# Block-sorted attention and a gated MLP on one core: the next batch's attention woven into this batch's gMLP in a fixed order

## The chip, the cores and the metric

The kernel runs on one core of a Trainium2 chip. The metric is the device time of one execution in microseconds. Before the change the median of three runs is 314.42 us (314.01 to 315.52).

## What is computed

Four batches, 8 heads, 768 tokens, head width 64; the tokens of a head form 8 blocks of 96. An 8x8 matrix per head (`sort_net`, after five rounds of exp and row and column scaling) mixes the blocks of K and of V. Each block of Q then attends to its mixed block. The heads side by side are the input x (768x512) of a gated MLP with a spatial matrix over the tokens.

```python
for _ in range(5):
    P = np.exp(P - np.max(P, axis=-1, keepdims=True))
    P = P / np.sum(P, -1, keepdims=True);  P = P / np.sum(P, -2, keepdims=True)
k_sorted = np.einsum('bhij,bhjcd->bhicd', P, k_b);  v_sorted = ...   # the same for v
attn = softmax(scale * q_b @ k_sb.T)          # 96x96 in each of the 8 blocks
x = (attn @ v_sb) as [batch, token, head*64]
h = np.maximum(x @ w_in, 0.0);  u, v = h[..., :512], h[..., 512:]
v_n = (v - mean(v)) / np.sqrt(var(v) + 1e-06)
v_s = np.einsum('ts,bsd->btd', w_spatial, v_n) + b_spatial[None, :, None]
out = (u * v_s) @ w_out
```

## The kernel before

**Layout.** A head's 768 tokens lie as 128 partitions of 6 tokens (token 6p+g in partition p, chunk g). With 96 = 16 x 6, a block is 16 partitions in all 6 chunks, so mixing the blocks is one matmul per chunk against a 128x128 matrix `pdiag` (32 of them, built on GpSimd at L192). The tile framework sorts the instructions of every engine by its own estimate of times; nothing in the code fixes the order. There are two PSUM pools (L67, L68): `ps2` with 2 buffers of two banks, `ps1` with 4 buffers of one bank.

**Start.** Weights are loaded first, on the GpSimd queue with a cast to bf16 (L116 to L131), then the heads. `w_spatial` is transposed on TensorE (L139, copies at L144). The 5 scaling rounds run on ScalarE and VectorE (L157 to L167).

**Attention of a batch (L223 to L284), head by head.** Three loads of 96 KB (L217, 128 rows of 1536 bytes in fp32 each). Six transposes of Q into `qt_ps` (L232, 64 partitions) and a copy that puts the tokens into block order (L236, VectorE). Six matmuls mix and transpose K (L240) and ScalarE copies them (L246). Six matmuls mix V (L250), VectorE copies (L257), and V goes to DRAM (L260) and comes back with a block's 96 tokens on partitions (L265, rows of 128 bytes); SyncE issues both. Eight matmuls of 64x96 by 96 columns give the scores (L272), ScalarE takes exp of all (L279). No maximum is subtracted.

**Softmax sums (L286 to L300).** Sixteen matmuls over the heads collect the sums of all 8 heads on 8 partitions (L289, L293). Two reciprocals on VectorE invert them (L299 512 wide, L300 256 wide). For each pair of heads two matmuls spread them over 128 partitions (L306, L308), ScalarE copies (L311), 16 matmuls of P·V in pairs on the two column halves of the array (L315, L321) give x transposed, and VectorE multiplies (L328) into `xt`.

**gMLP of the batch.** Per 128 tokens: v half of x·w_in (L340, 4 matmuls of 512 columns), relu (L347, ScalarE), mean and variance (L350, L351, VectorE). Then `rstd` through Ln and Exp on ScalarE (L354, L356), and 6 normalisations (L359, VectorE). Per 128 features: u (L370), relu (L377), spatial product and bias (L382, L388), gate (L396, VectorE). Per 128 tokens: output projection (L402), copy (L409, ScalarE), store (L410, SyncE).

```python
recip = small.tile([H, S], BF16, tag="recip")
nc.vector.reciprocal(out=recip[:, 0:512], in_=rs_a)
...
nc.scalar.activation(out=rstd, in_=mv_tile[:, :, 1], func=AF.Ln, bias=eps_tile[:], scale=1.0)
nc.scalar.activation(out=rstd, in_=rstd, func=AF.Exp, bias=0.0, scale=-0.5)
```

Of the kernel before, what the change touches and what calls it, by code (L numbers as in the profile page):

```python
# [21 lines left out]


@with_exitstack
def kernel(
# [17 lines left out]
    G = S // 128  # L44
    BH = B * H
# [22 lines left out]
    ps1 = ctx.enter_context(tc.tile_pool(name="ps1", bufs=4, space=bass.MemoryType.PSUM))  # L68
# [18 lines left out]
        out=sel16.rearrange("p (j t) -> p j t", t=16),  # L87
        in_=sel16.rearrange("p (j t) -> p j t", t=16),
        pattern=[[1, NB], [0, 16]], compare_op=ALU.not_equal,
        fill=1.0, base=0, channel_multiplier=-1,  # L90
    )

    selh = const.tile([BLK, H, H], BF16)
    nc.gpsimd.memset(selh, 0.0)
    nc.gpsimd.affine_select(
        out=selh, in_=selh, pattern=[[1, H], [-1, H]], compare_op=ALU.not_equal,
        fill=1.0, base=0, channel_multiplier=0,
    )

    ibc = const.tile([8, H * 64], BF16)  # L100
    nc.gpsimd.memset(ibc, 0.0)
    nc.gpsimd.affine_select(
        out=ibc.rearrange("p (h r) -> p h r", r=64),
        in_=ibc.rearrange("p (h r) -> p h r", r=64),
        pattern=[[1, H], [0, 64]], compare_op=ALU.not_equal,
        fill=1.0, base=0, channel_multiplier=-1,
    )

    ones_bf = const.tile([128, 128], BF16)
    nc.gpsimd.memset(ones_bf, 1.0)  # L110
# [5 lines left out]
    nc.gpsimd.dma_start(  # L116
        out=w_in_sb,
        in_=moe_w_in.rearrange("(kc p) f -> p kc f", p=128),
    )
    wsp_nat = pers.tile([128, SC, S], BF16)  # L120
    nc.gpsimd.dma_start(
        out=wsp_nat,
        in_=moe_w_spatial.rearrange("(tc p) s -> p tc s", p=128),
    )
    w_out_sb = pers.tile([128, FC, DM], BF16)
    nc.gpsimd.dma_start(
        out=w_out_sb,
        in_=moe_w_out.rearrange("(fc p) n -> p fc n", p=128),
    )
    b_sb = pers.tile([1, S], BF16)  # L130
    nc.gpsimd.dma_start(  # L131
        out=b_sb, in_=moe_b_spatial.rearrange("(a s) -> a s", a=1),
    )

    wspT = pers.tile([128, SC, S], BF16)
    for sc in range(SC):
        tp = ps1.tile([128, S], BF16, name="wspT_ps", tag="a")
        for tci in range(SC):
            nc.tensor.transpose(  # L139
                tp[:, tci * 128:(tci + 1) * 128],  # L140
                wsp_nat[:, tci, sc * 128:(sc + 1) * 128],
                ident_bf,
            )
        nc.vector.tensor_copy(out=wspT[:, sc, :], in_=tp)  # L144

    mask16_ps = ps1.tile([128, 128], FP32, name="mask16_ps", tag="a")
    nc.tensor.matmul(mask16_ps, lhsT=a16, rhs=a16, start=True, stop=True)
    mask16 = const.tile([128, 128], BF16)
    nc.vector.tensor_copy(out=mask16, in_=mask16_ps)

    p_all = pers.tile([BH, NB, NB], FP32)
    nc.sync.dma_start(out=p_all, in_=sort_net.rearrange("b h i j -> (b h) i j"))
# [30 lines left out]
    prep_ps = ps1.tile([128, NB * BH], FP32, name="prep_ps", tag="a")
    nc.tensor.matmul(prep_ps, lhsT=sel16, rhs=pt_sb, start=True, stop=True)
    prep_sb = pers.tile([128, NB * BH], BF16)
    nc.vector.tensor_copy(out=prep_sb, in_=prep_ps)

    pdiags = []
    for bh in range(BH):
        pd = pdiag_pool.tile([128, 128], BF16, name="pdiag")  # L190
        in1 = _raw_ap(prep_sb, bh, [prep_sb.ap[0], [BH, NB], [0, 16]])
        nc.gpsimd.tensor_mul(  # L192
            out=pd.rearrange("p (i t) -> p i t", t=16),
            in0=mask16.rearrange("p (i t) -> p i t", t=16),
            in1=in1,
        )
        pdiags.append(pd)

    def perm_in_ap(x: bass.AP, b: int, h: int) -> bass.AP:
        base = (b * H + h) * S * D  # L200
        return _raw_ap(x, base, [[6 * D, 128], [D, G], [1, D]])

    def blockview(ap, i):
        return ap[:, i * BLK:(i + 1) * BLK]

    def chunk2block(ap):
        return ap.rearrange("p (m j t) -> p j t m", m=G, j=NB, t=16)

    def natview(ap):
        return ap.rearrange("p (j t m) -> p j t m", j=NB, t=16, m=G)  # L210

    def expview(ap, i):
        return ap.rearrange("p (i c) -> p i c", c=BLK)[:, i, :]

    def load_perm(x: bass.AP, b: int, h: int, name: str, tag: str) -> bass.AP:
        t = att_in.tile([128, G, D], BF16, name=name, tag=tag)
        nc.gpsimd.dma_start(out=t, in_=perm_in_ap(x, b, h))  # L217
        return t

    for b in range(B):  # L220
        exp_tiles = []
        vblk_tiles = []
        for h in range(H):  # L223
            bh = b * H + h
            parity = h % 2
            q_perm = load_perm(q, b, h, "q_perm", "q")
            k_perm = load_perm(k, b, h, "k_perm", "k")
            v_perm = load_perm(v, b, h, "v_perm", "v")

            qt_ps = ps1.tile([64, G * 128], BF16, name="qt_ps", tag="a")  # L230
            for g in range(G):
                nc.tensor.transpose(  # L232
                    qt_ps[:, g * 128:(g + 1) * 128], q_perm[:, g, :], ident_bf,
                )
            qt_sb = att_mid.tile([64, S], BF16, name="qt_sb", tag="qt")
            nc.vector.tensor_copy(out=natview(qt_sb), in_=chunk2block(qt_ps))  # L236

            kt_ps = ps2.tile([64, S], FP32, name="kt_ps", tag="a")
            for g in range(G):
# [203 lines left out]
```

## Time and profile before

| | before |
|---|---|
| median of 3 runs | 314.42 us |
| span of the profiled execution | 313.4 us (its own time is given by no other number) |
| TensorE busy | 236.8 us, 76% |
| VectorE / ScalarE / GpSimd busy | 130.2 / 115.5 / 69.1 us |
| mean granted TensorE clock | 0.804 |
| chain that ended last | TensorE 61%, ScalarE 11%, VectorE 10%, DMA 8%, GpSimd 6% |

The span runs from the first to the last instruction; the run's time lies some 1 us above it. The granted clock is a share of 2.4 GHz; its two levels are 1.0 (2.4 GHz) and 0.5 (1.2 GHz), and a number between is a mean over the stretch. "Busy" of TensorE counts matmuls whose ends are modelled, so the time between the starts of neighbours says more than the duration of one.

### The profile page before, as it was taken

Reading aid. Unit: us, or ns where it says so; the run is one execution under the profiler, and the core shown is the slowest. Engines: PE = TensorE matmul, PEld = TensorE weight load, DVE = VectorE, ACT = ScalarE, POOL = GpSimd, SP = SyncE. Lnnn points to the kernel's source line nnn. Section 1 sums busy time; section 2 is a strip of 40 time slices with the busy share of each in tenths; the row PEclk is TensorE's granted clock in tenths of the full one; section 3 lists DMA queues with packets and bytes.
Section 4 is the critical chain, followed back from the end, with each engine's and each line's share of the span. In section 5 each row is a group of like instructions: output and inputs, shape, how many; then the busy total and the mean of one; then the engine's idle time right before and its main releaser. Section 6 shows DMA issues by size and latency. Waiting matters only on the chain.

```text
span 313.4 us, 4510 instructions
## 1 busy us (share of the span) xinstructions
PE 236.8 (76%) x1783; PEld 126.6 (40%) x1783; DVE 130.2 (42%) x216; ACT 115.5 (37%) x166; POOL 69.1 (22%) x149
## 2 busy tenths in 40 slices
PE   0058379489499997497699984794999983986994
PEld 0056265234144574143244762241445751432441
DVE  4345341533512382726321854536123917262220
ACT  2003333234512576126223664327125761353114
POOL 9239986100000285000000771000002100000000
PEclk9995955556779999658799997567799995586799
DMA  2996499400000599500001999100005950000005
GB/s 36 206 201 111 79 170 216 69 2 0 0 0 2 205 196 216 91 0 0 0 2 60 247 200 172 32 2 0 0 0 200 176 105 0 2 1 0 0 2 201
DMA packets 48917, 25.08 MB, mean 80 GB/s; under 512 B 27648, under 2 KB 45312, under 8 KB 48896
## 3 DMA queue, kind: packets, MB, share of 16 engines
q0 software_dynamic: 15696, 12.20, 26.1%
q1 hardware_dynamic: 33200, 12.60, 15.4%
q8 instruction: 14, 0.23, 0.3%
q14 instruction: 7, 0.06, 0.0%
HBM read 27.54 MB, written 9.44 MB: 118 GB/s over the span
## 4 chain that ended last, share of the span: by engine, by line
PE 61%; ACT 11%; DVE 10%; DMA 8%; POOL 6%; issue 2%; DVEq 0%; ACTq 0%; POOLq 0%
PE vst_ps L382 13%; PE v_ps L340 10%; PE ut_ps L370 7%; PE o_ps L402 7%; DMA w_out_sb<-in_moe_w_out_dram 5%; PE sc_ps L272 5%; DVE recip L299 4%; POOL pdiag L192 4%; PE vst_ps L388 3%; PE qt_ps L232 3%; PE ot_ps L315 3%; PE kt_ps L240 2%; ACT kt_sb L246 2%; ACT exp_sb L279 2%; PE rs_a L289 2%
## 5 line engine op out<-in xcount | busy, mean ns | idle before, releaser
L382 PE MATMUL vst_ps<-wspT,v_sb 128*128 128x512 bf16 (+1 forms) x192 | 46.1, 371 | 18.5 <-DVE v_sb L359 17.9
L217 POOL DMA_DIRECT2D q_perm<-in_q_dram x32 | 17.9, 560 | 156.1 <-PE qt_ps L232 153.0
L279 ACT ACTIVATE exp_sb<-sc_ps 96x768 bf16<-96x768 f32 x32 | 25.8, 806 | 36.7 <-PE sc_ps L272 36.7
L236 DVE COPY qt_sb<-qt_ps 64x768 bf16<-64x768 bf16 x32 | 30.2, 945 | 19.7 <-PE qt_ps L232 19.6
L396 DVE TENSOR_TENSOR gt_sb<-vst_ps,ut_sb 128x768 bf16<-128x768 f32 x16 | 15.3, 958 | 53.2 <-PE vst_ps L388 53.2
L382 PEld LDWEIGHTS <-v_sb 128*128 128x128 bf16 x192 | 19.4, 108 | 39.5 <-DVE v_sb L359 22.8
L340 PE MATMUL v_ps<-w_in_sb,xt 128*128 128x512 bf16 x96 | 35.1, 512 | 0.0
L377 ACT ACTIVATE ut_sb<-ut_ps 128x768 bf16<-128x768 f32 x16 | 13.0, 810 | 56.4 <-PE ut_ps L370 56.4
L246 ACT CAST kt_sb<-kt_ps 64x768 bf16<-64x768 f32 x32 | 25.1, 784 | 16.9 <-PE kt_ps L240 16.8
L370 PE MATMUL ut_ps<-xt,w_in_sb 128*128 128x512 bf16 (+1 forms) x128 | 31.2, 363 | 0.0
L311 ACT CAST bc_sb<-bc_ps 128x768 bf16<-128x768 f32 x16 | 12.8, 799 | 41.7 <-PE bc_ps L308 41.7
L328 DVE TENSOR_TENSOR xt<-ot_ps,bc_sb 128x768 bf16<-128x768 f32 x16 | 15.3, 958 | 28.4 <-PE ot_ps L321 23.2
L299 DVE RECIPROCAL recip<-rs_a 8x512 bf16<-8x512 f32 x4 | 13.4, 3346 | 26.1 <-PE rs_a L289 26.1
L257 DVE CAST vperm_sb<-vperm_ps 128x384 bf16<-128x384 f32 x32 | 17.4, 544 | 14.1 <-PE vperm_ps L250 8.7
L272 PE MATMUL sc_ps<-qt_sb,kt_sb 64*96 64x96 bf16 x256 | 19.7, 223 | 4.0 <-ACT kt_sb L246 3.5
L306 PE MATMUL bc_ps<-recip,ibc 8*128 8x512 bf16 x16 | 9.4, 591 | 16.6 <-DVE recip L299 13.1
L402 PE MATMUL o_ps<-w_out_sb,gt_sb 128*128 128x512 bf16 x96 | 21.4, 379 | 0.0
L315 PEld LDWEIGHTS <-vblk_sb 96*64 96x64 bf16 x128 | 10.9, 161 | 24.2 <-issue 24.2
L272 PEld LDWEIGHTS <-kt_sb 64*96 64x96 bf16 x256 | 15.5, 133 | 11.5 <-ACT kt_sb L246 9.1
L232 PE MATMUL qt_ps<-ident_bf,q_perm 128*64 128x128 bf16 x192 | 19.2, 239 | 1.0 <-DMA q_perm<-in_q_dram 1.0
L409 ACT COPY o_sb<-o_ps 128x512 f32<-128x512 f32 x24 | 13.7, 586 | 17.1 <-PE o_ps L402 17.1
L217 POOL DMA_DIRECT2D k_perm<-in_k_dram x32 | 17.7, 554 | 10.1 <-PE kt_ps L240 5.5
(73 smaller groups left out, 307.9 us busy)
## 6 DMA issues: line engine op xcount, KB each, us to landing
out_dram<-o_sb SPq DMA_DIRECT2D x24, 256.0 KB, 2.2
q_perm<-in_q_dram POOLq DMA_DIRECT2D x32, 96.0 KB, 4.9
k_perm<-in_k_dram POOLq DMA_DIRECT2D x32, 96.0 KB, 4.9
v_perm<-in_v_dram POOLq DMA_DIRECT2D x32, 96.0 KB, 4.9
vdram<-vperm_sb SPq DMA_DIRECT2D x32, 96.0 KB, 3.7
vblk_sb<-vdram SPq DMA_DIRECT2D x32, 96.0 KB, 3.1
wsp_nat<-in_moe_w_spatial_dram POOLq DMA_DIRECT2D x1, 1152.0 KB, 13.2
w_in_sb<-in_moe_w_in_dram POOLq DMA_DIRECT2D x1, 1024.0 KB, 8.6
```

Source lines behind the costliest of these rows:

```text
L217: nc.gpsimd.dma_start(out=t, in_=perm_in_ap(x, b, h))
L232: nc.tensor.transpose(qt_ps[:, g * 128:(g + 1) * 128], q_perm[:, g, :], ident_bf,)
L236: nc.vector.tensor_copy(out=natview(qt_sb), in_=chunk2block(qt_ps))
L246: nc.scalar.copy(out=natview(kt_sb), in_=chunk2block(kt_ps))
L272: nc.tensor.matmul(sc_ps[:, i, 0:BLK], lhsT=blockview(kt_sb, i), rhs=blockview(qt_sb, i), start=True, stop=True,)
L279: nc.scalar.activation(out=exp_sb.rearrange("p (i c) -> p i c", c=BLK), in_=sc_ps[:, :, 0:BLK], func=AF.Exp, scale=scale,)
L299: nc.vector.reciprocal(out=recip[:, 0:512], in_=rs_a)
L315: nc.tensor.matmul(ot_ps[0:64, i, 0:BLK], lhsT=vblk_tiles[2 * m][:, i, :], rhs=expview(exp_tiles[2 * m], i), start=True, stop=True,)
L340: nc.tensor.matmul(v_ps, lhsT=xt_tiles[kc][:, sc * 128:(sc + 1) * 128], rhs=w_in_sb[:, kc, DH:DFF], start=(kc == 0), stop=(kc == KC - 1),)
L370: nc.tensor.matmul(ut_ps[:, off:off + wdt], lhsT=w_in_sb[:, kc, mc * 128:(mc + 1) * 128], rhs=xt_tiles[kc][:, off:off + wdt], start=(kc == ...
L382: nc.tensor.matmul(vst_ps[:, off:off + wdt], lhsT=v_tiles[sc][:, mc * 128:(mc + 1) * 128], rhs=wspT[:, sc, off:off + wdt], start=(sc == 0) ...
L402: nc.tensor.matmul(o_ps, lhsT=gt_tiles[mc][:, sc * 128:(sc + 1) * 128], rhs=w_out_sb[:, mc, :], start=(mc == 0), stop=(mc == FC - 1),)
```

## The change

The kernel is rewritten, with the same mathematics.

- **Order.** `attention(b)` is a list of 28 units, `gmlp(b)` one of 14. Inside `manual_schedule` TensorE, VectorE and ScalarE run their instructions in the order in which the code issues them. First comes `attention(0)` alone, with the six transposes of `w_spatial` as units between its last ones. Then for every batch each gMLP unit is followed by two (at places three) attention units of the next batch. The last gMLP stands alone. GpSimd and SyncE are still sorted by the framework.
- **PSUM.** One pool of 4 buffers of two banks; every unit takes one buffer.
- **Loads.** Per batch one DMA for V, one for K (1024 rows of 1536 bytes each) and six for Q (1024 rows of 256 bytes each, as tokens x heads). Batch 0 is loaded ahead of the weights, batch 1 behind them, batch b+2 when stage b is issued.
- **Token order.** Q stays in the permuted order; blocks are picked by strided views (`block_cols`). `w_spatial`, the bias and the output rows are permuted in the same way.
- **Attention.** Two heads share a transpose (12 transposes of 128x128 per `qtr`) and a `ktr` (12 matmuls in column pairs). V is mixed by 8 matmuls of 384 columns, gets a column of ones per head (65 wide) and makes one round trip through DRAM per batch: one store, six reads (rows of 1040 bytes). `attend` gives x with tokens on partitions and the sum in column 64; VectorE takes 8 reciprocals per partition and multiplies. `xtr` transposes x on TensorE.
- **gMLP.** Two 128-token chunks share one PSUM buffer and one relu or copy (1024 wide); u and spatial products go in 384-column halves; the bias matmul has 128 rows instead of 1.
- **ScalarE.** One activation table set is named at the start (`preload_act_table_set`).

```diff
+    nc.scalar.preload_act_table_set("natural_log_exp_and_others")
+    def load_tokens(x, b, name):
+        t = ld.tile([128, G, H, D], BF16, name=name, tag=name)
+        for g in range(G):
+            nc.gpsimd.dma_start(
+                out=t[:, g],
+                in_=_raw_ap(x, b * H * S * D + g * D, [[G * D, 128], [S * D, H], [1, D]]),
+            )
...
+        def vmix(hp):
+            t = ps_tile()
+            for hh in range(2):
                 nc.tensor.matmul(
+                    t[:, hh, 0:G * D], lhsT=pd[:, 2 * hp + hh, :], rhs=v_in[:, 2 * hp + hh, :],
+                    start=True, stop=True,
                 )
...
+        def attend(n):
...
+            for hh in range(2):
+                for ii in range(NB // 2):
+                    i = ih * (NB // 2) + ii
+                    nc.tensor.matmul(
+                        t[0:BLK, hh, ii * VW:(ii + 1) * VW],
+                        lhsT=e[:, hh, ii, :], rhs=st["vb"][:, i, 2 * hp + hh, :],
+                        start=True, stop=True,
+                    )
+            tv = t[0:BLK, :, 0:NB // 2 * VW].rearrange("p h (i d) -> p h i d", d=VW)
+            rec = small.tile([BLK, 2, NB // 2], FP32, name="rec", tag="rec")
+            nc.vector.reciprocal(out=rec, in_=tv[:, :, :, D])
+            nc.vector.tensor_mul(
...
+        order = [
+            (vmix, 0), (vmix, 1), (vmix, 2), (vmix, 3), (qtr, 0), (ktr, 0), (qtr, 1), (ktr, 1),
+            (score, 0), (ktr, 2), (score, 1), (ktr, 3), (attend, 0), (score, 2), (attend, 1),
+            (score, 3), (attend, 2), (score, 4), (attend, 3), (score, 5), (attend, 4), (score, 6),
+            (xtr, 0), (attend, 5), (score, 7), (attend, 6), (attend, 7), (xtr, 1),
+        ]
...
+        order = (
+            [(vproj, n) for n in range(3)] + [(uproj, n) for n in range(FC)]
+            + [(spatial, n) for n in range(FC)] + [(oproj, n) for n in range(3)]
+        )
...
+    with tc.manual_schedule(engines=ORDERED):
...
+        for b in range(B):
+            if b + 2 < B:
+                load_batch(b + 2)
+            m_units = gmlp(b)
+            a_units = attention(b + 1) if b + 1 < B else []
+            done = 0
+            for n, unit in enumerate(m_units):
+                unit()
+                want = min(len(a_units), (n + 1) * 28 // 13)
+                while done < want:
+                    a_units[done]()
+                    done += 1
```

## Rows read from the trace of the kernel before

**Rows 1.** The page, busy time of each engine.

```profile
PE 236.8 (76%) x1783; PEld 126.6 (40%) x1783; DVE 130.2 (42%) x216; ACT 115.5 (37%) x166; POOL 69.1 (22%) x149
```

**Rows 2.** Windows: stretch and length, busy per engine, PEclk, DMA share, GB/s.

```profile
41.20:57.70 16.50, 15.52 (x115) 10.27 (x116) 4.34 (x6) 7.20 (x9) 10.67 (x21) 0.50 1.27 195
...
107.00:125.60 18.60, 16.20 (x223) 11.91 (x220) 11.06 (x16) 12.46 (x17) 12.70 (x24) 1.00 1.22 214
125.60:133.80 8.20, 3.54 (x39) 1.85 (x37) 5.92 (x3) 1.60 (x2) 0.00 (x0) 0.58 0.44 80
133.80:144.60 10.80, 10.80 (x58) 4.05 (x57) 3.37 (x4) 2.72 (x5) 0.00 (x0) 0.53 0.00 0
144.60:151.60 7.00, 2.54 (x14) 1.08 (x11) 4.09 (x14) 6.02 (x9) 0.00 (x0) 0.95 0.00 0
151.60:168.00 16.40, 16.19 (x81) 7.54 (x82) 4.45 (x8) 2.43 (x3) 0.00 (x0) 0.92 0.00 1
```

**Rows 3.** Groups by line: count, busy us, mean ns, idle before and its releasers.

```profile
L299 DVE RECIPROCAL recip<-rs_a 8x512 bf16<-8x512 f32 x4 | 13.4, 3346 | 26.1 <-PE rs_a L289 26.1
...
L354 ACT ACT_TABLE_LOAD x4 | 5.1, 1283 | 0.1
...
L377 ACT ACTIVATE ut_sb<-ut_ps 128x768 bf16<-128x768 f32 x16 | 13.0, 810 | 56.4 <-PE ut_ps L370 56.4
...
L347 ACT ACTIVATE v_sb<-v_ps 128x512 bf16<-128x512 f32 x24 | 12.7, 605 | 18.3 <-PE v_ps L340 18.2
...
L396 DVE TENSOR_TENSOR gt_sb<-vst_ps,ut_sb 128x768 bf16<-128x768 f32 x16 | 15.3, 958 | 53.2 <-PE vst_ps L388 53.2
...
L144 DVE COPY wspT<-wspT_ps 128x768 bf16<-128x768 bf16 x6 | 3.2, 556 | 8.2 <-PE wspT_ps L139 7.9
...
L350 DVE BATCH_NORM_STATS2 stats<-v_sb 128x6 f32<-128x512 bf16 x24 | 15.7, 669 | 8.9 <-ACT v_sb L347 8.9
...
L359 DVE TENSOR_SCALAR v_sb<-v_sb,mv_tile,rstd 128x512 bf16<-128x512 bf16 x24 | 8.1, 407 | 10.7 <-ACT rstd L356 10.7
...
L159 DVE RECIPROCAL rowsum<-rowsum 32x8 f32<-32x8 f32 x5 | 1.0, 191 | 0.2
```

**Rows 4.** Timeline at clock 1.0, TensorE: start us, us, what.

```profile
108.69 0.56 PE L272 MATMUL sc_ps<-qt_sb,kt_sb 64*96 64x96 bf16 x8
...
109.17 0.52 PE L240 MATMUL kt_ps<-pdiag,k_perm 128*64 128x128 bf16 x6
...
109.53 0.44 PE L232 MATMUL qt_ps<-ident_bf,q_perm 128*64 128x128 bf16 x5
...
109.91 0.35 PE L250 MATMUL vperm_ps<-v_perm,pdiag 128*128 128x64 bf16 x6
```

**Rows 5.** The chain that ended last, one piece: start us, us, what.

```profile
167.98 5.29 PE o_ps L402 x24
```

**Rows 6.** Timeline at clock 0.5: one column pair of P·V.

```profile
62.31 0.28 PE L315 MATMUL ot_ps<-exp_sb,vblk_sb 96*64 96x96 bf16 x1
62.32 0.28 PE L321 MATMUL ot_ps<-exp_sb,vblk_sb 96*64 96x96 bf16 x1
```

**Rows 7.** DMA queues in 111 to 125 us (q0) and in 250 to 259 us (q1).

```profile
q0 software_dynamic: 2902, 1.98, 96.4%
...
q1 hardware_dynamic: 5197, 0.97, 54.7%
```

**Rows 8.** The start: last scaling step (timeline); DMA issues, median us to landing.

```profile
10.97 0.21 DVE L167 TENSOR_TENSOR p_all<-p_all,colsum 32x64 f32<-32x64 f32 x1
...
vdram<-vperm_sb SPq DMA_DIRECT2D x32, 96.0 KB, 3.7
vblk_sb<-vdram SPq DMA_DIRECT2D x32, 96.0 KB, 3.1
wsp_nat<-in_moe_w_spatial_dram POOLq DMA_DIRECT2D x1, 1152.0 KB, 13.2
w_in_sb<-in_moe_w_in_dram POOLq DMA_DIRECT2D x1, 1024.0 KB, 8.6
```

More of the change, by code (lines that the diff above doesn't have):

```diff
@@ L95 @@
[L95 to L109, printed above, removed]
@@ L130 @@
[L130 to L144, printed above, removed]
@@ L146 @@
-    mask16_ps = ps1.tile([128, 128], FP32, name="mask16_ps", tag="a")
-    nc.tensor.matmul(mask16_ps, lhsT=a16, rhs=a16, start=True, stop=True)
+    e0 = const.tile([128, 128], BF16)
+    nc.vector.memset(e0, 0.0)
+    nc.vector.memset(e0[0:1, :], 1.0)
+    b_ext = pers.tile([128, S], BF16)
+    nc.vector.memset(b_ext, 0.0)
+    nc.vector.tensor_copy(
+        out=b_ext[0:1, :].rearrange("a (g p) -> a g p", g=G),
+        in_=b_nat.rearrange("a (p g) -> a g p", g=G),
+    )
+    vm_tiles = []
@@ L188 @@
[L188 to L201, printed above, removed]
@@ L220 @@
[L220 to L239, printed above, removed]
+    nc.vector.tensor_copy(out=prep_sb, in_=prep_ps[:, 0, 0:NB * BH])
@@ new lines, with make_pdiag @@
+    pdiag = {}
+    def make_pdiag(b, eng, parts=1):
+        pd = pd_pool.tile([128, H, NB, TB], BF16, name="pdiag")
+        n = H // parts
+        for x in range(parts):
+            eng.tensor_mul(
+                out=pd[:, x * n:(x + 1) * n],
+                in0=_raw_ap(mask16, 0, [mask16.ap[0], [0, n], [TB, NB], [1, TB]]),
+                in1=_raw_ap(prep_sb, b * H + x * n, [prep_sb.ap[0], [1, n], [BH, NB], [0, TB]]),
+            )
+        pdiag[b] = pd.rearrange("p h i t -> p h (i t)")
@@ new lines, with wsp_unit, block_cols @@
+    make_pdiag(0, nc.vector, 2)
+    wspT = pers.tile([128, G, S], BF16)
+    def wsp_unit(gs):
+        tp = ps_tile(BF16)
+        for go in range(G):
+            nc.tensor.transpose(
+                tp[:, 0, go * 128:(go + 1) * 128],
+                wsp_nat[:, go, :].rearrange("p (s g) -> p g s", g=G)[:, gs, :],
+                ident_bf,
+            )
+        nc.vector.tensor_copy(out=wspT[:, gs, :], in_=tp[:, 0, 0:S])
+    def block_cols(ap2d, i):
+        return ap2d.rearrange("p (g i t) -> p i g t", g=G, i=NB)[:, i]
@@ L268 @@
[L268 to L278 removed]
+            nc.scalar.copy(
+                out=vm[:, :, 2 * hp:2 * hp + 2, 0:D].rearrange("p g h d -> p h g d"),
+                in_=t[:, :, 0:G * D].rearrange("p h (g d) -> p h g d", g=G),
+            )
@@ new lines, in qtr @@
+        def qtr(n):
+            t = ps_tile(BF16)
+            q_sb = qk_pool.tile([128, 2, S], BF16, name="qT", tag="q", bufs=3)
+            for x in range(2):
+                hp = 2 * n + x
+                for g in range(G):
+                    nc.tensor.transpose(
+                        t[:, x, g * 128:(g + 1) * 128],
+                        q_in[:, g, 2 * hp:2 * hp + 2, :].rearrange("p h d -> p (h d)"),
+                        ident_bf,
+                    )
+                st["q", hp] = q_sb[:, x, :]
+            nc.vector.tensor_copy(out=q_sb, in_=t[:, :, 0:S])
@@ L353 @@
-        rstd = small.tile([128, SC], FP32, tag="rstd")
-        nc.scalar.activation(out=rstd, in_=mv_tile[:, :, 1], func=AF.Ln,
-                             bias=eps_tile[:], scale=1.0)
-        nc.scalar.activation(out=rstd, in_=rstd, func=AF.Exp, bias=0.0,
-                             scale=-0.5)
-        for sc in range(SC):
-            nc.vector.tensor_scalar(
-                out=v_tiles[sc], in0=v_tiles[sc],
-                scalar1=mv_tile[:, sc, 0:1], scalar2=rstd[:, sc:sc + 1],
-                op0=ALU.subtract, op1=ALU.mult,
-            )
@@ new lines, in xtr @@
+        def xtr(n):
+            t = ps_tile(BF16)
+            xt = xt_pool.tile([128, 2, S], BF16, name="xt", tag="xt")
+            for x in range(2):
+                kc = 2 * n + x
+                for i in range(NB):
+                    nc.tensor.transpose(
+                        t[:, x, 0:S].rearrange("p (g i t) -> p i g t", g=G, i=NB)[:, i],
+                        st["x"][:, i, kc * 128:(kc + 1) * 128],
+                        ident_bf[0:BLK, 0:BLK],
+                    )
+                xts[b, kc] = xt[:, x, :]
+            nc.vector.tensor_copy(out=xt, in_=t[:, :, 0:S])
@@ new lines, in attention, with gmlp, vproj @@
+        order = [
[4 more added lines that the diff above has]
+        ]
+        return [lambda f=f, a=a: f(a) for f, a in order]
+    def gmlp(b):
+        st = {"v": [], "gt": []}
+        def vproj(n):
+            t = ps_tile()
+            for x in range(2):
+                g = 2 * n + x
+                for kc in range(KC):
@@ new lines, in vproj @@
+            if n == G // 2 - 1:
+                rstd = small.tile([128, G], FP32, name="rstd", tag="rstd")
+                nc.scalar.activation(
+                    out=rstd, in_=st["mv"][:, :, 1], func=AF.Ln, bias=eps_tile[:], scale=1.0,
+                )
+                nc.scalar.activation(out=rstd, in_=rstd, func=AF.Exp, bias=0.0, scale=-0.5)
+                for g in range(G):
+                    nc.vector.tensor_scalar(
+                        out=st["v"][g], in0=st["v"][g],
+                        scalar1=st["mv"][:, g, 0:1], scalar2=rstd[:, g:g + 1],
+                        op0=ALU.subtract, op1=ALU.mult,
+                    )
@@ L388, with spatial @@
+        def spatial(mc):
+            t = ps_tile()
+            for g in range(G):
+                for x in range(2):
+                    nc.tensor.matmul(
+                        t[:, x, 0:HW], lhsT=st["v"][g][:, mc * 128:(mc + 1) * 128],
+                        rhs=wspT[:, g, x * HW:(x + 1) * HW],
+                        start=(g == 0), stop=False,
+                    )
+            for x in range(2):
                 nc.tensor.matmul(
-                    vst_ps[:, off:off + wdt],
-                    lhsT=ones_bf[0:1, 0:128],
@@ new lines, in spatial, with oproj @@
+            nc.vector.tensor_mul(
+                out=gt.rearrange("p (x c) -> p x c", x=2), in0=t[:, :, 0:HW],
+                in1=st["u", mc].rearrange("p (x c) -> p x c", x=2),
+            )
+            st["gt"].append(gt)
+        def oproj(n):
+            t = ps_tile()
+            for x in range(2):
+                g = 2 * n + x
+                for mc in range(FC):
+                    nc.tensor.matmul(
+                        t[:, x, :], lhsT=st["gt"][mc][:, g * 128:(g + 1) * 128],
+                        rhs=w_out_sb[:, mc, :],
+                        start=(mc == 0), stop=(mc == FC - 1),
+                    )
+            o_sb = o_pool.tile([128, 2, DM], FP32, name="o_sb", tag="o")
+            nc.scalar.copy(out=o_sb, in_=t)
```

336 lines of the change are left out of this document (151 added, 185 removed).

## The prediction

> **What bounds the kernel now.** I read the busy line first, then windows cut along one batch, then groups and timeline for prices. No engine is full: TensorE 76%, all others under 45% [rows 1]. A batch takes 66.5 us, in stages with different limits (batch 1, [rows 2]; the sixth stage, the output projection, is [rows 5]):
>
> - 18.6 us of attention, TensorE busy 16.2 us at clock 1.0.
> - 8.2 us around the softmax sums: TensorE busy 3.5 us, behind a reciprocal of 3.35 us [rows 3] and a second one half as wide. The clock falls to its lower level.
> - 10.8 us of P·V and the v projection: TensorE 100% busy at a mean clock of 0.53. Half of this stage is the price of the gap before it.
> - 7.0 us of normalisation: TensorE busy 2.5 us, ScalarE 6.0, two activation table loads of 1.28 us among them [rows 3].
> - 16.4 us of u, spatial product and gate at 0.92, then 5.3 us of output projection at full rate [rows 5].
>
> So the bound is TensorE, made long by serial chains (sums, normalisation) and by the low clock that follows them. Batch 0's attention runs wholly at 0.50 though 94% busy [rows 2], and starts at about 41 us, behind the weights.
>
> **TensorE's work per batch after the change.** In [rows 5], 24 matmuls of 512 columns take 5.29 us: 0.43 ns a column. The gMLP streams 58,368 columns (v, u and output projection 12,288 each, spatial 18,432, bias 3,072): 25.1 us; with unit edges I take 25.4. Attention goes by the starts in [rows 4]: a score 60 ns (0.48 us for 8), a K matmul 60 (0.36 for 6), a transpose 76 (0.38 for 5).
>
> - vmix: 8 x 384 columns, 1.3 us.
> - qtr: 24 transposes at 76 ns, 1.8 us (before 48).
> - ktr: 48 matmuls as 24 column pairs. Unseen for K, but two column halves start 10 ns apart in [rows 6]. Bounds: 24 x 72 = 1.7 us in pairs (60 ns plus 12 for wider loads), 48 x 60 = 2.9 us in line. I take 1.7.
> - score 64 x 60 = 3.8 us. attend 64 matmuls of 65 columns, nearest the score: 3.8 us; from below their columns alone, 1.8 us; from above a transpose's pitch, 4.9.
> - xtr: 32 transposes of 96 columns at 72 ns, 2.3 us.
>
> That is 14.7, in all 40.1 us. Gone are 16 sum matmuls, 8 spreading matmuls and half the Q transposes. The bias matmul has 128 rows but the same columns: nothing.
>
> **The other engines hide beside that.** ScalarE at 605 ns for 512 columns and 810 for 768 [rows 3] (0.8 ns a column, so 1.02 us for 1024): 8 exp, 4 K copies, 4 V copies and 4 relus of u at 0.81, 6 of 1024, 0.5 for rstd: 22.8 us. VectorE: 4 gates 3.8, 4 copies of 1536 bf16 at 0.96 (twice the columns of the 556 ns row), 8 x (0.19 + 0.69) in attend (0.69 is the gate's 0.96 less 256 columns), 6 statistics 5.0 with aggregates, 6 normalisations 2.4: 22.0 us. Both are half of TensorE, so their busy time costs nothing; if TensorE ran at 20 us they would bind. GpSimd's three later pdiags (32 before) are wanted only after 50 us: nothing.
>
> **The new waits.** (1) In a fixed order, behind vproj 2 ScalarE holds Ln and Exp ahead of ktr 0's copy, and VectorE holds six normalisations ahead of qtr 0's copy. From the end of vproj 2: relu 1.2, statistics 1.5, rstd 0.8, normalisations 2.0 to 2.4, Q copy 1.0, so qtr 0's buffer is free at 6.5 to 6.9. TensorE has qtr 0, ktr 0, uproj 0, qtr 1 in the four buffers (3.9 us) and ktr 1 waits 2.6 us. (2) At the end xtr 1 waits for two attends' divisions: 1.5 us. (3) Small waits, where three units of ScalarE's work (2.6 us) stand beside 2.4 us of TensorE's: 1.2 us. A warm stage: 40.1 + 2.6 + 1.5 + 1.2 = **45.4 us**.
>
> Wait (1) rests on the table loads being gone. Before, each Ln and each Exp behind it reloads [rows 3]; whether naming one set ends that, no row shows. Bounds: nothing, or 2.6 us more in wait (1) per stage, some 10 us in all. I take nothing, as the program asks for one set. The Trainium skill (ScalarE: Activation LUTs, Table sets: the hidden batching unit) says that one set holds both exp and ln; by it the sum stays, without it the sum would be 10 us more.
>
> **V's round trip.** 96 KB went out in 3.7 us and back in 3.1 [rows 8]. 780 KB go out once and come back in six parts: I estimate 9 to 12 us, mostly bytes at the 200 KB per us of the loads. Between vmix 3 and attend 0 stand vproj 2, four uprojs, qtr, ktr and two scores: about 14 us. Hidden; uncovered it would cost up to 5 us in the stage whose loads run beside it. SyncE's stores wait in order with it, and nobody waits for those.
>
> **The Q loads.** A batch takes 8 issues on GpSimd instead of 24, but Q becomes 6,144 packets of 128 bytes written, 384 per DMA engine. Price of one: 15 ns on SyncE's queue (54.7% of 9 us on 16 engines, 5,197 packets of mean 187 bytes), 74 ns on GpSimd's queue (96.4% of 14 us, 2,902 packets of mean 682 bytes) [rows 7]. So 5.8 to 28 us. The 74 ns are mostly bytes (9 bytes per ns), so I take 20 ns: 8 us. The Trainium skill (DMA: Bandwidth & Descriptors, Specifications) asks for at least 512 B per transfer and says that below it the engine reads, modifies and writes; that speaks against this load, and by it the price stands at the upper bound.
>
> **The start.** w_in's 1 MB landed 8.6 us after its issue and the 1.15 MB behind it 4.6 us later or a little more [rows 8]: about 4 us of start and 230 KB per us. V, issued at 3 us, lands at 10.5, K at 14, Q at 22, the weights by 36 (V's round trip adds 6), batch 1 by 58. Scaling ends at 11.2 [rows 8]; with five short steps and pdiag on VectorE vmix starts at 15, and V is back at about 33. From Q on, TensorE has qtr to xtr and 36 transposes: at the low clock, as batch 0 now [rows 2], and at 1.6 times the prices above some 26 us. Waits for V and behind the divisions add 6. attention(0) ends at **54 us**.
>
> **Sum.** 54, then stage 0 with 45.4 + 7 (up to 14 us of low clock at its start, as the dense 10.8 us stage shows [rows 2], costs half of that), two stages of 45.4, then the last gMLP: 25.4 + 0.5 wait + 4.6 for copy and store = 30.5. Together 227.7 us against the span of 313.4. The run's time lies 1.0 above the span, as the median 314.4 does now: **228.7 us**.
>
> **Rivals.**
> - *The clock sags in every stage.* For it: the 7.0 us stage ends in a fall, and dense work stays at 0.53 for 10 us [rows 2]. Against: 18.6 us of small matmuls hold 1.0 with 87% busy, and the new waits are shorter. At the 0.85 that batch 1 averages over its stages [rows 2, 5], 40.1 becomes 47.2 and a stage 53: 54 + 3 x 53 + 35 + 1 = 249 us.
> - *Q's packets cost the upper bound.* 28 us instead of 8: attention(0) ends 16 us later, at 70. Batch 1's Q lands at 95 but is wanted at 77: 17 us more. Later batches have a stage of lead. 262 us.
> - *The weaving hides little.* This is the change not doing what it says: units wait for each other as stages do now. Then a stage is the present 18.6 of attention plus 25.4 plus the 7.0 gap = 51 [rows 2]: 228.7 + 3 x 5.6 = 246 us, all of it from what was removed.
> - *Slower: the clock never rises.* For it: batch 0's attention, 94% busy, at 0.50 throughout, and 100% busy at 0.53 [rows 2]. Transposes and small matmuls now stand in every stage. Then gMLP is 50 us and attention 14.7 x 1.6 = 24, a stage 79, the last 56: 54 + 4 + 3 x 79 + 56 = 351 us. It decides where a stage passes 72 us, a mean clock of about 0.57. Against: the same small work at 1.0 in batch 1.
>
> **Chances.** Forecast 0.57, sagging clock 0.15, Q packets 0.13, little weaving 0.09, slower 0.04, no change 0.02. The low end is every wait covered: start 48, stage 0 45, two of 42, last 29 = 206. 257 takes in the sagging clock and little weaving, with 8 us of V's round trip or the table loads on top, and leaves out Q at its upper bound. So faster by over 0.5% (about what a measurement of this kernel can tell from no change) 0.94, within 0.02, slower 0.04.
>
> **What would show it.** Right: the mean clock above 0.9 after 70 us, TensorE over 85% busy in the middle stages, no table load after the first, starts of the stages 44 to 48 us apart, ktr's starts in pairs, one wait of 2 to 3 us per stage behind the normalisation. Wrong: the first qtr after 30 us or batch 1's qtr waiting for its load (Q packets); attend 0 waiting for V; windows at clock 0.5 inside the later stages; TensorE waiting for ScalarE or VectorE in more than a fifth of a stage.

## The result and the profile after

The changed kernel takes 234.39 us (231.19 to 235.66), the kernel before 314.97 us beside it: a ratio of 0.736, 95% interval 0.728 to 0.744. Medians here take in every run, while ratios and their intervals go by the fast runs alone (of this kernel 231.19 and 233.40 us; its other two ran in the slower state). The forecast was 228.7 us. The profiled execution took 233.4 us, span 231.4, so 2.0 us lie around the span; beside the experiments, runs of the kernel before lie 1.7 to 1.8 us above their spans, not the 1 us that was taken.

The page of the changed kernel, its busy line, TensorE's busy tenths and granted clock in 40 slices of 5.8 us, and the chain that ended last:

```profile
PE 168.5 (73%) x1551; PEld 105.3 (46%) x1559; DVE 98.8 (43%) x216; ACT 88.3 (38%) x118; POOL 38.8 (17%) x50
PE   0069000199896707999997599989895999899990
PEclk9999855555699955999999979999998899999997
PE 49%; DMA 28%; ACT 8%; DVE 7%; SPq 4%; issue 2%; DVEq 0%; ACTq 0%
```

TensorE is busy 68 us less than in [rows 1], yet 73% of the shorter span is a smaller share than the 76% before. The zeros in slices 5 to 7 and 15 and the 5s in slices 23 and 31 show where it stands still; the clock falls behind each. The chain names the cause: DMA went from 8% to 28%.

The changed kernel's four stages in windows, cut at the starts of the v projections (columns as in [rows 2]):

```profile
60.50:112.10 51.60, 39.67 (x376) 24.12 (x377) 22.94 (x43) 20.43 (x27) 7.05 (x8) 0.89 0.82 108
112.10:156.20 44.10, 39.34 (x376) 23.81 (x377) 21.17 (x42) 21.34 (x28) 0.00 (x0) 0.96 0.28 73
156.20:200.40 44.20, 39.23 (x375) 23.68 (x376) 21.16 (x42) 21.34 (x28) 0.00 (x0) 0.96 0.27 73
200.40:231.40 31.00, 24.98 (x136) 13.11 (x135) 10.76 (x22) 10.43 (x13) 0.00 (x0) 0.96 0.17 68
```

Against the forecast, term by term: attention(0) ended at 60.5 (54 forecast), stage 0 took 51.6 (52.4), stages 1 and 2 44.1 and 44.2 (45.4 each), the last gMLP 31.0 (30.5). The miss is the start. But the stages came out right by two errors that cancel, as the next views show. First the waits of the changed kernel's engines (us in total, times, longest), then TensorE's timeline (in brackets the idle time before and what ended it):

```profile
PE ps L316 <- DMA vb<-vd: 35.7, 4, 21.7
```
```profile
45.24 0.82 PE L316 MATMUL ps<-vb,ex 96*96 96x65 bf16 x8 [21.74 <-DMA vb<-vd]
...
122.87 0.53 PE L274 MATMUL ps<-pdiag,k_in 128*64 128x128 bf16 x12 [0.91 <-ACT kT L281]
...
127.33 0.39 PE L294 MATMUL ps<-qT,kT 64*96 64x96 bf16 x8
127.65 0.53 PE L274 MATMUL ps<-pdiag,k_in 128*64 128x128 bf16 x12
128.10 1.47 PE L393 MATMUL ps<-xt,w_in_sb 128*128 128x384 bf16 x8
132.26 0.52 PE L316 MATMUL ps<-vb,ex 96*96 96x65 bf16 x8 [2.68 <-DMA vb<-vd]
```

All four batches wait for V at attend 0, 35.7 us in all: 21.7 in the start, 8.4 in stage 0, 2.7 and 2.9 in the others. Wait (1), forecast as 2.6 us behind the normalisation, is 0.91, and it ends with ScalarE's copy of the first K, not with VectorE's copy of Q. Prices are lower too: eight scores take 0.32 us up to the next start (40 ns each, 60 forecast), a ktr 0.45.

What a wait costs behind itself stands in windows of the changed kernel (the wait for V, then the work behind it):

```profile
23.40:45.20 21.80, 0.11 (x4) 0.00 (x0) 0.00 (x0) 2.19 (x4) 9.49 (x7) 0.59 1.24 213
45.20:60.50 15.30, 15.26 (x181) 13.97 (x182) 10.78 (x23) 4.84 (x6) 6.13 (x7) 0.50 1.83 181
80.00:88.00 8.00, 0.05 (x1) 0.08 (x2) 0.00 (x0) 0.39 (x1) 0.00 (x0) 0.62 1.42 174
...
129.60:132.30 2.70, 0.04 (x2) 0.07 (x2) 0.00 (x0) 0.82 (x2) 0.00 (x0) 1.00 0.41 44
132.30:136.00 3.70, 3.70 (x32) 2.36 (x33) 1.78 (x4) 0.81 (x1) 0.00 (x0) 0.62 0.02 4
```

After 2.7 us of idling the next 3.7 us run at a mean of 0.62, after 21.8 us the next 15.3 us at 0.50 though fully busy. The trip itself is in the changed kernel's chain of waits (start us, us, what; first batch 0's V, then batch 1's, then batch 2's):

```profile
15.92 0.83 PE ps L237 x2
16.78 2.94 ACT vm L241 x4
19.74 12.30 DMA vd<-vm
...
34.33 10.83 DMA vb<-vd
45.24 0.82 PE ps L316 x8
...
68.07 8.48 DMA vd<-vm
...
78.81 9.01 DMA vb<-vd
...
118.89 5.15 DMA vd<-vm
...
126.37 5.80 DMA vb<-vd
132.26 0.52 PE ps L316 x8
133.78 3.40 PE ps L408 x12
...
138.29 1.95 PE ps L408 x12
```

With no bulk loads beside it (batch 2's) the trip is 13.4 us: 5.15 out, 2.3 for SyncE's issues, one behind the other, and 5.80 for the last read. Beside them it is 19.9 us, in the start 25.5 us. Behind the wait the first spatial product takes 3.40 us, where the next takes 1.95.

### The profile page after: what moved, and what is told of

Its sections match the earlier page's. It is cut to its first block, busy times and chain, and to the rows that moved or that the text cites. A ratio compares the mean times of both kernels' runs of the same rounds, so it can differ in the third digit from the quotient of the medians.

```text
span 231.4 us, 3676 instructions
## 1 busy us (share of the span) xinstructions
PE 168.5 (73%) x1551; PEld 105.3 (46%) x1559; DVE 98.8 (43%) x216; ACT 88.3 (38%) x118; POOL 38.8 (17%) x50
## 4 chain that ended last, share of the span: by engine, by line
PE 49%; DMA 28%; ACT 8%; DVE 7%; SPq 4%; issue 2%; DVEq 0%; ACTq 0%
PE ps L408 15%; DMA vb<-vd 14%; DMA vd<-vm 13%; PE ps L430 9%; PE ps L316 7%; ACT vm L241 5%; PE ps L362 4%; PE ps L294 4%; SPq L250 4%; PE ps L337 3%; PE ps L414 2%; PE ps L393 2%; DVE x_sb L324 2%; PE ps L215 2%; ACT v_sb L370 2%
## 5 line engine op out<-in xcount | busy, mean ns | idle before, releaser
L301 ACT ACTIVATE ex<-ps 96x768 bf16<-96x768 f32 x32 | 25.8, 806 | 74.4 <-PE ps L294 74.4
L316 PE MATMUL ps<-vb,ex 96*96 96x65 bf16 x256 | 19.7, 232 | 35.7 <-DMA vb<-vd 35.7
L408 PE MATMUL ps<-wspT,v_sb 128*128 128x384 bf16 x192 | 38.1, 354 | 0.0
L316 PEld LDWEIGHTS <-ex 96*96 96x96 bf16 x256 | 17.4, 148 | 39.2 <-issue 33.9
L419 DVE TENSOR_TENSOR gt<-ps,u_sb 128x768 bf16<-128x768 f32 x16 | 15.3, 957 | 26.0 <-PE ps L414 24.4
L99 POOL DMA_DIRECT2D q_in<-in_q_dram x24 | 21.1, 892 | 16.8 <-DMA wsp_nat<-in_moe_w_spatial_dram 7.3
L373 DVE BATCH_NORM_STATS2 stats<-v_sb 128x6 f32<-128x512 bf16 x24 | 16.3, 677 | 17.4 <-ACT v_sb L370 17.3
L393 PE MATMUL ps<-xt,w_in_sb 128*128 128x384 bf16 x128 | 23.0, 327 | 0.6 <-ACT u_sb L399 0.6
L362 PE MATMUL ps<-w_in_sb,xt 128*128 128x512 bf16 x95 | 22.6, 382 | 0.6 <-DVE xt L343 0.6
L430 PE MATMUL ps<-w_out_sb,gt 128*128 128x512 bf16 x89 | 22.2, 380 | 0.8 <-DVE gt L419 0.5
L324 DVE TENSOR_TENSOR x_sb<-ps,rec 96x512 bf16<-96x512 f32 x32 | 22.0, 686 | 1.1
L362 PEld LDWEIGHTS <-xt 128*128 128x128 bf16 x96 | 9.3, 99 | 11.3 <-DVE xt L343 1.1
L281 ACT CAST kT<-ps 128x768 bf16<-128x768 f32 x16 | 12.7, 794 | 1.5 <-PE ps L274 1.5
```

Source lines behind the costliest of these rows:

```text
L99: nc.gpsimd.dma_start(out=t[:, g], in_=_raw_ap(x, b * H * S * D + g * D, [[G * D, 128], [S * D, H], [1, D]]),)
L301: nc.scalar.activation(out=e.rearrange("p h i c -> p h (i c)"), in_=t[0:BLK, :, 0:NB // 2 * BLK], func=AF.Exp, scale=scale,)
L316: nc.tensor.matmul(t[0:BLK, hh, ii * VW:(ii + 1) * VW], lhsT=e[:, hh, ii, :], rhs=st["vb"][:, i, 2 * hp + hh, :], start=True, stop=True,)
L324: nc.vector.tensor_mul(out=x_sb[:, ih * (NB // 2):(ih + 1) * (NB // 2), hp * 128:hp * 128 + 128] .rearrange("p i (h d) -> p h i d", h=2), ...
L362: nc.tensor.matmul(t[:, x, :], lhsT=xts[b, kc][:, g * 128:(g + 1) * 128], rhs=w_in_sb[:, kc, DH:DFF], start=(kc == 0), stop=(kc == KC - 1),)
L373: nc.vector.bn_stats(out=stats, in_=v_sb[:, x, :])
```

## Experiments

**Theory A:** V's round trip bounds the start and the stages; what waits for it also pays in clock. Rivals: the start is bound by w_spatial's load (**B**), the stages by ScalarE and VectorE between the normalisation and K's copies (**C**), and the weaving itself does little (**D**).

**Attend without V's wait.** The program does the whole round trip, but P·V reads a constant, so that the output is not the attention's.

```diff
+    vb_const = pers.tile([BLK, NB, H, VW], BF16, name="vb_const")
+    nc.gpsimd.memset(vb_const, 1.0)
...
-    lhsT=e[:, hh, ii, :], rhs=st["vb"][:, i, 2 * hp + hh, :],
+    lhsT=e[:, hh, ii, :], rhs=vb_const[:, i, 2 * hp + hh, :],
```

> P·V reads a constant tile instead of the mixed V that came back from DRAM; the round trip itself still runs, so only the wait for it goes (the output is not attention's). Theory: V's round trip is the wait that ends last, 21.7 us in the start, 8 us in stage 0 and 2.7 us in stages 1 and 2, with some 5 us of low clock behind them; without it about 198 us (193 to 205), the rest being waits for batch 1's loads. Rival: the wait only covers other lateness (weights, batch 1's Q, ScalarE), which then ends last: above 222 us.

Measured 199.72 us (ratio 0.632, 0.624 to 0.639). Windows of this kernel's first two stages:

```profile
47.50:87.80 40.30, 37.66 (x377) 23.15 (x377) 22.23 (x44) 20.22 (x27) 15.25 (x17) 1.00 1.73 192
87.80:127.30 39.50, 37.42 (x375) 23.19 (x376) 21.07 (x42) 21.23 (x28) 0.00 (x0) 1.00 0.43 102
```

So V's wait, with the clock behind it, costs 33.7 us between the spans (231.4 and 197.7): 13.0 in the start, 11.3 in stage 0, 4.6 in each of the stages 1 and 2. The same 376 matmuls then run at clock 1.00. B has a share only now: in the start TensorE waits 6.1 us for w_spatial, which V's wait had covered (this kernel's waits):

```profile
PE ps L217 <- DMA wsp_nat<-in_moe_w_spatial_dram: 6.1, 1, 6.1
```

**V in two halves.** Four heads each: store, six reads and a tile of its own, so that attend 0 to 3 need the first half alone.

```diff
-            if hp == HP - 1:
+            if hp % 2 == 1:
+                half = hp // 2
...
-                nc.sync.dma_start(out=vd, in_=vm.rearrange("p g h d -> p (g h d)"))
+                nc.sync.dma_start(out=vd, in_=vm[half].rearrange("p g h d -> p (g h d)"))
...
-                st["vb"] = vb
+                st["vb", half] = vb
```

> The round trip in two halves of 4 heads, the first starting after vmix 1. Theory: attend 0 needs only the first half, which leaves 2.5 us earlier and has half the bytes: the waits of stages 1 and 2 go (2.7 us each and about 1.7 us of low clock), stage 0 gains about 5 us, the start 3 to 6: about 217 us (212 to 223). Rival (the trip is not what ends last, or its fixed parts dominate): 229 to 235 us.

Measured 206.99 us (0.654, 0.646 to 0.663), below the range given: the start gains 7.5 us where 3 to 6 were expected, stage 0 gains 8.6 where 5 were. The waits of this kernel and windows of its first two stages:

```profile
PE ps L320 <- DMA vb<-vd: 15.6, 2, 14.9
```
```profile
53.00:96.00 43.00, 38.74 (x376) 23.33 (x378) 22.85 (x43) 20.44 (x27) 7.04 (x8) 0.96 1.41 156
96.00:135.60 39.60, 37.51 (x376) 23.20 (x376) 21.09 (x42) 21.23 (x28) 0.00 (x0) 1.00 0.26 82
```

Batch 0 waits 14.9 us, batch 1 0.7, the later ones not at all, and stages 1 and 2 are as short as with a constant V. A kernel that leaves nothing out thus gets 25.6 of the 33.7 us (span 205.8).

**V one stage earlier.** V of batch b+2 is mixed at the end of stage b, batch 1's inside attention(0). For that the later `pdiag`s are built ahead of attention(0).

```diff
-            (vmix, 0), (vmix, 1), (vmix, 2), (vmix, 3), (qtr, 0), (ktr, 0), (qtr, 1), (ktr, 1),
+            (qtr, 0), (ktr, 0), (qtr, 1), (ktr, 1),
...
+                if n >= 7 and v_next:
+                    v_next.pop(0)()
```

> The four vmix units of batch b+2 stand at the end of stage b (those of batch 1 inside attention(0)), so that the round trip has half a stage of cover; the start's own trip is untouched. Theory: the waits of all three stages go (8 + 3 us in stage 0, 4.4 in each of the others) and attention(0) grows by about 3 us of vmix work: about 215 us (210 to 221); attend 0 of batch 0 still starts at about 45 us. Rival: stages stay at 44 us because wait (1) or the evacuations take its place: 227 us or more.

Measured 215.77 us (0.681, 0.666 to 0.695), as A expects. The one wait for V left is the start's:

```profile
PE ps L316 <- DMA vb<-vd: 22.1, 1, 22.1
```

Then both diffs together:

> Both: the trip in halves, and vmix a stage early. Theory: the stages no longer wait for V either way, so early vmix adds nothing to the halves except its 3 us in attention(0): 205 to 210 us. Rival (stage 0's trip, still contended, costs the halves several us): 200 to 204 us.

Measured 207.62 us (0.657, 0.652 to 0.662), no less than the halves alone: either edit frees the later stages, and once is enough.

**Bulk loads held behind V.** w_spatial, w_out and batch 1 are issued only when batch 0's V is back (GpSimd in fixed order, behind a one-element copy out of `vb`).

```diff
-    nc.gpsimd.dma_start(out=wsp_nat, in_=moe_w_spatial.rearrange("(p g) s -> p g s", g=G))
-    nc.gpsimd.dma_start(out=w_out_sb, in_=moe_w_out.rearrange("(fc p) n -> p fc n", p=128))
-    load_batch(1)
...
+    def late_loads(vb):
+        nc.gpsimd.tensor_copy(out=wsp_nat[0:1, 0, 0:1], in_=vb[0:1, 0, 0, 0:1])
+        nc.gpsimd.dma_start(out=wsp_nat, in_=moe_w_spatial.rearrange("(p g) s -> p g s", g=G))
+        nc.gpsimd.dma_start(out=w_out_sb, in_=moe_w_out.rearrange("(fc p) n -> p fc n", p=128))
+        load_batch(1)
```

> Start alone: w_spatial, w_out and batch 1's loads are issued only when batch 0's V is back (GpSimd's order fixed, a copy of one element holds the queue). Theory: the trip takes 25 us in the start because it shares the DMA engines with the bulk loads; alone it takes about 13 us as in stages 1 and 2, so attend 0 starts at 33 to 36 us instead of 45. Batch 1's loads come later, which gives some of it back: 222 to 228 us. Rival (the start is bound by the sum of the bytes): attend 0 starts earlier but stage 0 waits by as much for batch 1: 230 to 236 us.

Measured 224.22 us (0.706, 0.681 to 0.732), inside the range. From its timeline, the first attends of batches 0 and 1:

```profile
33.68 0.82 PE L321 MATMUL ps<-vb,ex 96*96 96x65 bf16 x8 [7.59 <-DMA vb<-vd]
...
79.16 0.82 PE L321 MATMUL ps<-vb,ex 96*96 96x65 bf16 x8 [9.84 <-DMA vb<-vd]
```

Batch 0's trip falls from 25.5 to 12.5 us, and stage 0 begins at 51.0 instead of 60.5. So the bulk loads had doubled it. But the loads now run in stage 0, where batch 1's V waits 9.84 us: stage 0 takes 53.6 us, 2.0 of the 9.5 us given back.

**Halves with the loads held.** Only batch 0's loads go ahead of V; the order behind it is new. The held loads are issued as soon as V's first half is back.

```diff
+        nc.gpsimd.dma_start(out=wsp_nat, in_=moe_w_spatial.rearrange("(p g) s -> p g s", g=G))
+        nc.gpsimd.dma_start(out=w_in_sb, in_=moe_w_in.rearrange("(kc p) f -> p kc f", p=128))
+        load_batch(1)
+        nc.gpsimd.dma_start(out=w_out_sb, in_=moe_w_out.rearrange("(fc p) n -> p fc n", p=128))
```

> The halves, and in the start only Q, K and V of batch 0 are loaded ahead of V's return; then w_spatial, w_in, batch 1, w_out in the order of need. Theory: the first half is back at 28 to 31 us (38 with the halves alone, 45 in the changed kernel) and stage 0 starts at 45 to 48 us; batch 1's Q lands about when it is wanted: 197 to 202 us. Rival (the bytes bound the start): attend 0 at 30 us, but stage 0 waits for batch 1's K and Q: 204 to 209 us.

Measured 208.50 us (0.660, 0.653 to 0.667): a time of the rival's range, though nothing in stage 0 waits for K or Q. This kernel's timeline, then the window of its stage 0:

```profile
27.21 0.82 PE L325 MATMUL ps<-vb,ex 96*96 96x65 bf16 x8 [1.86 <-DMA vb<-vd]
35.27 0.81 PE L221 MATMUL ps<-ident_bf,wsp_nat 128*128 128x128 bf16 x6 [4.68 <-DMA wsp_nat<-in_moe_w_spatial_dram]
41.52 0.82 PE L325 MATMUL ps<-vb,ex 96*96 96x65 bf16 x8 [3.02 <-DMA vb<-vd]
72.23 0.82 PE L325 MATMUL ps<-vb,ex 96*96 96x65 bf16 x8 [3.87 <-DMA vb<-vd]
```
```profile
49.90:97.20 47.30, 40.59 (x381) 24.35 (x379) 22.56 (x44) 20.36 (x27) 13.66 (x16) 0.93 1.50 177
```

V's wait in the start shrinks to 1.86 and 3.02 us; the held w_spatial costs 4.68 and batch 1's V 3.87. The next kernel does two more things: w_spatial's transposes follow the last attention units, and batch 2's loads wait for batch 1's V.

```diff
-            if n >= 16 and n % 2 == 0:
+            if n >= 22:
...
+                if b == 0 and n == 2:
+                    hold = small.tile([1, 1], BF16, name="hold", tag="hold")
+                    nc.gpsimd.tensor_copy(out=hold, in_=vbs[-1][0:1, 0, 0, 0:1])
+                    load_batch(2)
```

> The gated start with halves, with the six w_spatial transposes after the last attention units and batch 2's loads held until stage 0's V is back. Theory: attention(0) loses its waits for w_spatial (4.7 us) and stage 0 its wait for V (3.9 us and the low clock behind it): 198 to 203 us. Rival (the bytes bound the start): the waits move to w_in and batch 1's K and Q: 205 to 210 us.

Measured 201.94 us (0.641, 0.636 to 0.646), the fastest of the kernels that leave nothing out, 2.2 us above the one that waits for no V. From its timeline, V's two waits in the start and the starts of stages 0 and 1:

```profile
27.06 0.52 PE L325 MATMUL ps<-vb,ex 96*96 96x65 bf16 x8 [2.81 <-DMA vb<-vd]
41.48 0.82 PE L325 MATMUL ps<-vb,ex 96*96 96x65 bf16 x8 [9.75 <-DMA vb<-vd]
...
51.86 0.38 PE L371 MATMUL ps<-w_in_sb,xt 128*128 128x512 bf16 x1
...
91.69 1.89 PE L371 MATMUL ps<-w_in_sb,xt 128*128 128x512 bf16 x8
```

The whole gain lies in stage 0, 39.8 us instead of 47.3. The start did not get shorter, against the theory: the wait for w_spatial is gone, but V's second half still comes back at 41.5 us, its wait grows from 3.02 to 9.75, and stage 0 begins 2.0 us later. The second half makes its trip beside the loads that the first half's return has let go; holding them until it is back was not tried. The two edits were not tried one by one either; that stage 0 alone gains speaks for the held batch 2.

**Unwoven.** Each stage runs all attention units, then all of gMLP.

```diff
-            for n, unit in enumerate(m_units):
+            for unit in a_units + m_units:
                 unit()
...
```

> In every stage all 28 attention units of the next batch come first, then the 14 gMLP units: same instructions, same fixed orders, nothing woven. Theory: V's trip (13 us, 20 in stage 0) has only some 5 us of cover left and the rest of attention is paced by its own chain of ScalarE, TensorE and VectorE, so a stage grows from 44 to about 55 us: 262 us (252 to 272). Rival (the gain came from what was removed and weaving hides little): 234 to 245 us.

Measured 271.23 us (0.859, 0.853 to 0.866); its waits for V are 64.4 us. D falls, but the run does not say what else the weaving hides. So the halves with early V were unwoven as well:

```diff
-            for n, unit in enumerate(m_units):
+            for unit in a_units + m_units + v_next:
                 unit()
...
```

> The kernel with halves and early vmix (207.6 us), unwoven: in each stage the attention units, then the gMLP units, then vmix; no wait for V is in the way. Theory: weaving by itself hides the waits of attention's chain and of the normalisation, 6 to 8 us a stage: 222 to 235 us. Rival (weaving only hid V's trip): 206 to 212 us.

Measured 240.41 us (0.763, 0.759 to 0.769), 32.8 above the same kernel woven and outside the range I gave: I had meant this run to be free of V's waits, and it is not. Its waits and windows of one gMLP and one attention:

```profile
PE ps L320 <- DMA vb<-vd: 34.6, 5, 14.0
```
```profile
81.30:107.10 25.80, 25.23 (x135) 13.39 (x136) 11.57 (x23) 8.40 (x11) 0.00 (x0) 0.98 0.08 23
107.10:130.40 23.30, 17.73 (x241) 14.77 (x240) 10.05 (x20) 12.95 (x17) 0.00 (x0) 0.70 0.37 115
```

Here gMLP and attention take 49.1 us against 40.3 woven. The gMLP by itself is 98% busy, so the normalisation leaves it no wait for the weaving to hide. Attention's 23.3 us hold 4.5 us of V's wait, and the mean clock over them is 0.70. Of the 32.9 us between the spans (238.7 and 205.8), 20.6 are waits for V behind the start; the rest is in part the clock behind them. How much weaving is worth where nothing waits for V stays open.

**Without the table set.** The line that names ScalarE's table set is left out, alone and together with the halves.

```diff
-    nc.scalar.preload_act_table_set("natural_log_exp_and_others")
```

> The line that names the activation table set is left out. Expected by the prediction's bound: two loads per batch return and each stage's normalisation chain is 2.6 us longer, some 10 us in all: about 244 us. Theory after the trace: in stages 0 to 2 attend 0 waits for V anyway and hides the loads; only the last gMLP, which has no such wait, pays about 2.6 us: 234 to 239 us. If no load returns: 231 to 235 us.

> The halves (207.0 us) without the line that names the table set. In the changed kernel the eight loads came back and cost nothing, hidden by the wait for V. Theory: here no such wait is left, so each normalisation chain is longer by up to 2.6 us and TensorE waits for it: 210 to 217 us. Rival (the chain has slack of its own): 205 to 209 us.

Alone it takes 229.96 us (0.727, 0.721 to 0.734), below all three times expected and no more than with the line; on the halves 211.34 us (0.673, 0.667 to 0.678), 4.4 more, as expected. Groups and the wait for V of the first, then the wait behind K's copy in the second and in the halves:

```profile
L377 ACT ACT_TABLE_LOAD x4 | 5.1, 1283 | 0.1
L380 ACT ACT_TABLE_LOAD x4 | 5.1, 1283 | 0.1
```
```profile
PE ps L315 <- DMA vb<-vd: 27.8, 3, 20.9
```
```profile
PE ps L277 <- ACT kT L284: 6.6, 3, 2.2
```
```profile
PE ps L278 <- ACT kT L285: 2.7, 3, 0.9
```

The eight loads return in both. Where attend waits for V anyway they cost nothing; where it doesn't, wait (1) grows by 1.3 us per stage, and the stage from 39.6 to 40.8. C is real, but small and covered. The span of the first kernel, 226.3 us, is even 5.1 below the changed one's: 1.5 of them lie in the start, 2.5 in stage 1 and 1.1 in stage 2. Its waits for V are 27.8 us instead of 35.7. The longer wait (1) stands between the store of V and attend 0 and so covers 1.3 us more of the trip; in stage 1 nothing waits for V any more, and the clock stays at 1.00. Why the trip itself is shorter there (12.5 us at most, against 13.4) is open, and the nearest runs of the two kernels lie only 0.6 us apart (230.58 and 231.19).

## Why the prediction came out as it did

**What failed: "Hidden" for V's round trip, and "V is back at about 33".** V was back at 45.2, and attend 0 waited for it in every stage. Three parts of the step were each off, and all on one side.

- The trip: 9 to 12 us estimated, 13.4 measured alone. The estimate was bytes over the bulk rate; the 2.3 us that SyncE's issues take one after another, up to the last read, were not in it.
- The cover: about 14 us were counted from the end of vmix 3. It was 12.7 us (116.9 to 129.6), and ScalarE's copy of V, done 2.0 us behind vmix, takes its share of it: 10.7 us from the store to attend 0. So 2.7 us stayed bare, and the 3.7 us behind them ran at 0.62.
- The loads beside it: "up to 5 us" was named for the stage with loads and left out of the sum, 8.4 came. In the start, V was to be back at 33, 13 us behind the store's measured start at 19.7; the trip took 25.5. Holding the loads back shows why (25.5 to 12.5 us).

**What offset it.** The first qtr began at 18.5 us, not 22, and attention(0)'s work was priced too high (26 us, against 20.2 measured: 4.9 ahead of V's wait, 15.3 behind it). So the wait for V, 21.8 us where 6 of waits were forecast, moved the end of attention(0) by 6.5 us only. In the stages the small matmuls cost less than forecast: 60 ns a score, 40 measured. In the kernel before scores start one by one, 45 ns apart, with longer gaps where the kind changes; in the changed kernel they start in pairs, some 14 ns apart and 45 ns from pair to pair. There a unit's two heads lie on the two row halves of the array, which fits the pairs; the prediction paired K's products only. Without V's wait a stage is 39.5 us, not 45.4: TensorE's work takes 37.4 us instead of 40.1, and the waits 2.1 instead of 5.3. V's wait and its clock gave 4.6 us back. Stage 0 was given 7 us of low clock; without V's wait it takes 40.3 us at 1.00, and the wait with its clock put 11.3 in its place. That one sum came right is no support for its terms.

**What held.** gMLP's price: the last stage took 31.0 us against 30.5. K's products run in pairs, 3 to 4 ns apart, and 12 take 0.45 us; in the kernel before they started some 55 ns apart, one by one. ScalarE's and VectorE's busy times, 22.8 and 22.0 us forecast, were 21.3 and 21.2 in stage 1. After 70 us the mean clock is 0.94, and TensorE is 89% busy in stages 1 and 2. One table load is left of nine, and without the named set the eight return: this was right as a fact, and worth nothing in this kernel. The Trainium skill (ScalarE: Activation LUTs, Table sets: the hidden batching unit) has both functions in one set; the runs agree, and add that here the set had to be named.

**Q's packets** cost less than taken in the sum (8 us). The DMA view of the changed kernel in 3 to 20 us (GB/s in slices of 0.425 us) shows V and K at 204 GB/s, then Q at 155; in the timeline the first qtr starts at 18.46:

```profile
GB/s 0 0 7 52 60 96 179 202 188 202 201 206 206 204 195 204 206 204 204 204 204 206 203 158 157 152 157 153 157 153 157 153 157 152 165 213 205 222 222 207
```

The slower part is 12 slices, 5.1 us, 13 ns for each of 384 packets of an engine: just below the lower bound of 15. The Trainium skill (DMA: Bandwidth & Descriptors, Specifications) asks for at least 512 B per transfer. By it the prediction named 28 us, against the 8 us that it took; in this trace the 128-byte writes lost a quarter of the rate.

**The rivals.** The clock does not sag by itself: without V's wait all three woven stages run at 1.00. Unwoven, the kernel takes 271 us (240 with halves and early V), and much of the difference is V's wait: the weaving hides at least that. The slower case had no sign.

## What to carry to other kernels

- In a fixed order a transfer is hidden only by the work that stands between its issue and its first use; count both ends, the copy ahead of it and the issues one behind the other, and price it beside the bulk loads that run then. Where cover and trip differ by a few us, the answer is "bare".
- Cut a round trip so that the first consumer needs its first part alone (25.6 us here), and issue bulk loads behind a transfer that somebody waits for; but look where the held loads land next.
- A wait that ends last hides the price of everything beside it: the table loads cost nothing until V's wait was gone, then 4.4 us. Test an edit's worth on the kernel without the wait.

## What was not expected of the hardware

- The same 780 KB store took 12.30 us beside bulk loads and 5.15 us without, its last read 10.83 against 5.80.
- A wait of 2.7 us cost 1.9 us more in clock (4.6 us in a stage); after 21.8 us of idling, 15.3 us of full work passed at the lower level.
- Matmuls of 64 rows and 96 columns started 45 ns apart at clock 1.00 in the kernel before, and two within 14 ns of each other where a unit's two heads lie on different row halves: 40 ns each instead of 60, with the changes of kind.
